# Sketched attention and a gated FFN on one core: weight loads in thirds, a two-step release of the later loads, casts and fills moved to ScalarE

## The chip, the cores and the metric

The kernel runs on 1 core of one Trainium2 chip. A core has TensorE (PE; its weight loads are shown as PEld), VectorE (DVE), ScalarE (ACT), GpSimd (POOL) and SyncE (SP), which issues transfers, and 16 DMA engines that carry all transfers. SP and ACT issue transfers whose descriptors are made by hardware; POOL's are made by its software and may change the type on the way. The metric is device microseconds of one execution, as the median of several runs.

## What is computed

Attention with a sketched kernel in place of the softmax, for 4 batches of 4 heads, 1088 positions and 32 dimensions, and behind it a gated FFN over 4352 tokens. In short:

```python
def phi(x):                                   # r = 8, so 64 features
    a = np.einsum('rd,bhsd->bhsr', S1, x)
    b = np.einsum('rd,bhsd->bhsr', S2, x)
    return np.einsum('bhsi,bhsj->bhsij', a, b).reshape(*x.shape[:-1], r * r)
q_p, k_p = (phi(q), phi(k))
kv = np.einsum('bhsf,bhsd->bhfd', k_p, v)
z = np.sum(k_p, axis=2)
num = np.einsum('bhsf,bhfd->bhsd', q_p, kv)
den = np.einsum('bhsf,bhf->bhs', q_p, z)[..., None] + 1e-06
attn = num / den
x = attn.transpose(0, 2, 1, 3).reshape(4352, 128)
gate = np.maximum(x @ w_gate, 0.0)            # w_gate, w_val: 128 x 1536
val = x @ w_val
out = gate * val @ w_out                      # w_out: 1536 x 128
```

All inputs and the output are float32 in memory; the FFN and the large products run in float16.

## The kernel before

Everything but the loads at the start is a `Task`: an engine, an expected time that the engine is taken (`occ`) and until the result is there (`lat`), tasks that it needs (`deps`) or only follows (`after`), PSUM banks, and an expected earliest time (`at`). `Plan.set_due` gives each task a due time, counted back from those of the FFN units with a slack of 200 ns at each step, and `Plan.run` puts the tasks in an order by list scheduling over the expected times: for each engine the task that can start first, or among those within 30 ns the one due first. The instructions are then written in that order. So all expected times (the `land` table of loads, `at`, `due`) only shape the order on each engine; on the chip an instruction waits for its engine's earlier instructions and for its data, and for no clock. Changing an expected time can therefore move work anywhere in the program.

The stages, for each batch b:

- Keys: DVE transposes `k_sb` to `kt` (L405), PE multiplies by the sketch `sk` (L415, two products), DVE transposes the result to `abk` (L427), PE sums for z (L474) and forms the denominator's weights (L491, DVE zd and wst), POOL makes the 64 features `kp` (L301; for batch 0 DVE makes a part, from a copy of `abk` in PSUM that ACT makes, L448), PE multiplies by `v_sb` (L513), and DVE puts the result into `kv_bd` (L528).
- Queries, in groups (batch 0 in chunks of 1, 1, 2 and 4, batches 1 to 3 in 8, one rest group at the end): DVE transposes `q_sb` to `qt` (L588, L590), PE multiplies by `wst` (L612), DVE transposes to `abq` (L627), bw, dn, rd and an normalise, DVE or POOL makes the features `qp` (L301), which are turned to `pt` by PE and ACT (L671, L712; batch 0 and the rest group) or by a transposing DMA (L701; batches 1 to 3), PE multiplies by `kv_bd` (L678, "num"), and ACT writes `xT` (L720).
- FFN, 102 units of 512 columns: PE multiplies by `wg` and `wv` (L747), ACT takes the relu (L758), DVE multiplies (L767), PE multiplies by `wo` (L778, "out"), and ACT evicts each finished group (L795), whose store SP issues.

Until the first FFN matmul, PE's planned gaps are filled with products of zeros (L824).

The loads. SP issues the first sketch half, k of batch 0 in two parts and q of batch 0 in one. POOL fills batch 1's constant parts (`fills`, L291 to L295: zeros in `wst`, the unused end of `v_sb`, of `kt` and `kv_bd`), issues v of batch 0, `wg` and `wv` whole, makes `kp` of batch 0, issues `wo` (L367), and fills for batches 2 and 3. The k and q of batches 1 to 3 are issued by SP, one behind the other, once POOL has written one element into `k_sb` of batch 1 (the gate):

```python
def e_gate(t):
    nc.gpsimd.memset(k_sb[1][0:1, 0, 0:1], 0.0)
    for b in range(1, B):
        load_pairs(nc.sync, k_sb[b], k, b)
        load_pairs(nc.sync, q_sb[b], q, b)
P.add("gate", "POOL", 70, 100, emit=e_gate, at=T_GATE).due = T_GATE
```

The v of batches 1 to 3 are issued by POOL among its arithmetic, and cast to float16 on the way.

Of the kernel before, what the change touches and what calls it, by code (L numbers as in the profile page):

```python
# [9 lines left out]
FP32 = mybir.dt.float32  # L10
# [28 lines left out]
class Plan:  # L39
# [4 lines left out]
    def __init__(self, free, a_max, f_max, n_banks):  # L44
        self.tasks = []
        self.free = dict(free)
        self.a_max, self.f_max, self.n_banks = a_max, f_max, n_banks
        self.sem = 45.0

    def add(self, *args, **kw):  # L50
        t = Task(*args, **kw)
        self.tasks.append(t)
        return t

    def set_due(self, slack):
        after = {}
        for t in self.tasks:
            for d in t.deps + t.after:
                after.setdefault(id(d), []).append(t)
        order, seen = [], set()  # L60

        def visit(t):
            stack = [(t, iter(after.get(id(t), ())))]
            seen.add(id(t))
            while stack:
                top, it = stack[-1]
                for n in it:
                    if id(n) not in seen:
                        seen.add(id(n))
                        stack.append((n, iter(after.get(id(n), ()))))  # L70
                        break
                else:
                    order.append(top)
                    stack.pop()

        for t in self.tasks:
            if id(t) not in seen:
                visit(t)
        for t in order:
            for n in after.get(id(t), ()):  # L80
                s = slack if n.kind != "f" or t.kind != "f" else 0.0
                t.due = min(t.due, n.due - t.lat - s)

    def run(self, first_f):
# [97 lines left out]
def kernel(  # L182
# [12 lines left out]
    nc = tc.nc  # L195

    B, H, S, D = q.shape
# [8 lines left out]
    CB = C - CA  # L206
    NG = 10
    NH = 14
    assert (B, H, D, R, C) == (4, 4, 32, 8, 17)

    ctx.enter_context(tc.manual_schedule())
# [11 lines left out]
    k_sb = [const.tile([128, 2, C * D], FP32, name=f"k_sb{b}") for b in range(B)]  # L223
    q_sb = [const.tile([128, 2, (C + 1) * D], FP32, name=f"q_sb{b}") for b in range(B)]
    v_sb = [const.tile([128, H, CA * D], FP16, name=f"v_sb{b}") for b in range(B)]
    wg = const.tile([DM, NJ, 128], FP16, name="wg")
    wv = const.tile([DM, NJ, 128], FP16, name="wv")
    wo = const.tile([128, NJ, DM], FP16, name="wo")

    def load_pairs(eng, dst, src, b, hp=None):  # L230
# [3 lines left out]
        else:  # L234
            eng.dma_start(out=dst[:, hp, 0:C * D], in_=x[:, hp])

    def load_v(eng, dst, b):
        x = v[b].rearrange("h (t c) d -> t h (c d)", c=C)
        eng.dma_start(out=dst[0:T], in_=x[:, :, 0:CA * D])
        eng.dma_start(out=dst[T:128, :, 0:CB * D], in_=x[:, :, CA * D:])  # L240
# [5 lines left out]
    load_pairs(nc.sync, q_sb[0], q, 0)  # L246

    zero = const.tile([128, 128], FP16, name="zero")
    nc.vector.memset(zero, 0.0)  # L249
# [38 lines left out]
        nc.vector.memset(maskkv[64 * p:64 * p + 64, p], KVSCALE)  # L288
    nc.vector.tensor_tensor(out=maskz, in0=mz2[:, 0], in1=mz2[:, 1], op=ALU.add)

    def fills(eng, b):  # L291
        eng.memset(wst[b], 0.0)
        eng.memset(v_sb[b][T:128, :, CB * D:], 0.0)
        eng.memset(kt[b][:, :, C], 0.0)
        eng.memset(kv_bd[b], 0.0)  # L295

    fills(nc.vector, 0)

    def outer(eng, dst, a, b):
        n = dst.shape[1]  # L300
# [4 lines left out]
            op=ALU.mult,  # L305
        )

    T0, STEP, T_GATE, T_DT = 12500.0, 830.0, 12500.0, 2500.0
    P = Plan(free={"PE": 1200.0, "ACT": 3100.0, "DVE": 3600.0, "POOL": 3000.0, "SP": 20000.0},
             a_max=3, f_max=5, n_banks=7)  # L310

# [6 lines left out]
    def pool(n):  # L318
        return dict(occ=70 + 1.86 * n, lat=120 + 1.86 * n)

    T_S = 4000.0
    land = dict(k00=4200.0, k01=4850.0, q0=6700.0, v0=8700.0, wg=10500.0, wv=13000.0, wo=16500.0,
                k1=17500.0, v1=20000.0, q1=20500.0, k2=22500.0, v2=23000.0, q2=24500.0, k3=26500.0,
                v3=26000.0, q3=28500.0)


    def e_st(t):
# [26 lines left out]
    t_w0 = [P.add("wst0", "ACT", 350, 480, deps=[t_st], after=[t_sk], emit=e_wst0, frees=[t_st])]  # L354

    def prep(b):
        f = P.add(f"fill{b}", "POOL", 800, 800, emit=lambda t: fills(nc.gpsimd, b))
        t_fill.append(f)
# [3 lines left out]
    t_fill = []  # L362
    t_w0 += [prep(b) for b in range(1, B)]


    def e_load(dst, src):
        return lambda t: nc.gpsimd.dma_start(out=dst, in_=src)  # L367

    l_v0 = P.add("ld_v0", "POOL", 1350, 1350, emit=lambda t: load_v(nc.gpsimd, v_sb[0], 0))
    l_g = P.add("ld_wg", "POOL", 740, 740, deps=[l_v0],  # L370
                emit=e_load(wg, moe_w_gate.rearrange("m (j f) -> m j f", j=NJ)))
    l_v = P.add("ld_wv", "POOL", 560, 560, deps=[l_g],
                emit=e_load(wv, moe_w_val.rearrange("m (j f) -> m j f", j=NJ)))
    l_o = P.add("ld_wo", "POOL", 1050, 1050, deps=[l_v],
                emit=e_load(wo, moe_w_out.rearrange("(j f) m -> f j m", f=128)))
    l_v_sb = [l_v0]
    l_v0.after += t_fill[:1]
    for f in t_fill[1:]:
        f.after.append(l_o)
    prev = l_o  # L380
    for b in range(1, B):
        prev = P.add(f"ld_v{b}", "POOL", 1350, 1350, deps=[prev, t_fill[b - 1]],
                     emit=lambda t, b=b: load_v(nc.gpsimd, v_sb[b], b), at=10000.0 + 3000.0 * b)
        prev.due = T0 - 1000.0 + 5000.0 * b
        l_v_sb.append(prev)

    def e_gate(t):
        nc.gpsimd.memset(k_sb[1][0:1, 0, 0:1], 0.0)
        for b in range(1, B):
            load_pairs(nc.sync, k_sb[b], k, b)  # L390
            load_pairs(nc.sync, q_sb[b], q, b)

    P.add("gate", "POOL", 70, 100, emit=e_gate, at=T_GATE).due = T_GATE


    class Keys:
# [2 lines left out]
    kk = []  # L399
    for b in range(B):  # L400
        K = Keys()
        kk.append(K)

        def ke_t1(t, b, hp):
# [114 lines left out]
        m = None  # L519
        for lo, hi in cuts:  # L520
            x = P.add(f"k{b}kv{lo}", "PE", 60 * (hi - lo), 60 * (hi - lo) + 200,
                      deps=[K.phi[lo, 0], K.phi[lo, 1], *K.v], after=[m], banks=0 if m else 1)
            m = m or x
            x.emit = lambda t, b=b, lo=lo, hi=hi, m=m: ke_kv(t, b, lo, hi, m)
        K.kv = x
# [41 lines left out]
    for i, (bs, c0, n, r, o0) in enumerate(groups):  # L567
        G = Group()
        gg.append(G)
        G.bs, G.c0, G.n = bs, c0, n  # L570
        X = 4 * n
        rest = len(bs) > 1
        early = i < 2
        turned = not rest and bs[0] > 0
# [118 lines left out]
        for c in range(0, n, 4):  # L693
            p = Part()
            G.parts.append(p)
            p.G, p.n, p.c0, p.col = G, min(n, 4), c, col
            col += p.n * 128
            need = phi if n <= 4 else phi[2 * (c // 4):2 * (c // 4) + 2]
            if turned:
                def qe_dt(t, G=G, c=c):  # L700
                    nc.sync.dma_start_transpose(  # L701
                        out=G.pt[:, 2 * c:2 * c + 8],
                        in_=G.qp[:, 4 * c:4 * c + 16].rearrange("s x f -> s (x f)"))

                tre = P.add(f"q{i}dt{c}", "SP", T_DT, T_DT + 1500, deps=need, after=[last_dt],
                            emit=qe_dt)
# [12 lines left out]
            p.x = P.add(f"q{i}x{c}", "ACT", **act(128 * p.n), deps=[num], frees=[num],  # L719
                        emit=lambda t, p=p, f=num: nc.scalar.copy(  # L720
                            out=xT[:, p.col:p.col + p.n * 128], in_=ps[:, f.bank, 0:p.n * 128]))
            before.setdefault(id(r), []).append(p.x)
# [8 lines left out]
    for gi, p in enumerate(p for G in gg for p in G.parts):  # L731
# [3 lines left out]
        for i in range(NJ // per):  # L735
# [9 lines left out]
            def e_mm(t, w, p=p, js=js, W=W):  # L745
                for y, j in enumerate(js):
# [5 lines left out]
            vv = P.add(f"v{u}", "PE", 218, 218 + 170, deps=[p.x, g], banks=1, kind="f",  # L752
                       emit=lambda t, f=e_mm: f(t, wv), at=land["wv"])
            g.due, vv.due = due, due + 220

            def e_relu(t, U, g):
# [102 lines left out]
```

## Time and profile before

| what | us |
|---|---|
| runs shown | 110.37, 110.91, 111.2 (median 110.91) |
| profiled execution, its own time | 110.49 |
| its span | 108.7 |
| PE busy (92% of the span) | 99.8 |
| DVE busy (84%) | 91.6 |
| ACT busy (66%) | 72.2 |
| POOL busy (47%) | 51.1 |
| first FFN matmul starts | 12.89 |
| wg, wv, wo landed | 12.40, 14.24, 16.40 |
| k of batch 1 issued, landed | 12.45, 19.53 |

Times inside the execution are counted from the span's start. The granted clock of TensorE is 1.00 in every stretch up to 106 us. An engine's share of busy time is an average over a head in which loads set the pace and a long stretch of FFN units; a wait is charged to what the profile infers as the last releaser. L numbers are lines of the kernel before; in the changed kernel the same statements stand 13 to 27 lines lower (L747 is L774, L778 is L805, L405 is L425).

### The profile page before, as it was taken

How to read it: one execution, taken by the hardware profiler on the slowest of the kernel's cores; microseconds unless marked ns; L12 is line 12 of the kernel's file. 1: busy time of each engine (PE TensorE's matmuls, PEld its weight loads, DVE VectorE, ACT ScalarE, POOL GpSimd, SP SyncE). 2: the span in 40 equal slices, each digit the busy share in tenths (PEclk: the TensorE clock that was granted, in tenths of full speed). 3: DMA queues.
4: the chain of work that ended last, by engine and by line, in shares of the span. 5: the costliest groups of instructions: out<-in, count | busy, mean ns of one | idle time of the engine just before them, and what ended most of it. 6: DMA issues, size and time to landing. Idle time of an engine off the chain costs nothing.

```text
span 108.7 us, 3081 instructions
## 1 busy us (share of the span) xinstructions
PE 99.8 (92%) x1175; PEld 66.7 (61%) x1175; DVE 91.6 (84%) x199; ACT 72.2 (66%) x140; POOL 51.1 (47%) x84
## 2 busy tenths in 40 slices
PE   6999978599999999999999999999999999999930
PEld 6778767187657554656576556565774666568710
DVE  4659973899999998999999799799995999889820
ACT  4330469168597619666978495499767989989910
POOL 6979898089829719503294088025925000000000
PEclk9999999999999999999999999999999999999997
DMA  1999999999912582100045440000471400400302
GB/s 38 319 184 158 156 221 300 309 310 311 222 31 48 103 99 54 42 0 6 0 96 113 86 96 3 0 0 11 106 148 30 103 0 0 99 1 6 82 14 48
DMA packets 14559, 10.75 MB, mean 99 GB/s; under 512 B 8657, under 2 KB 11345, under 8 KB 14545
## 3 DMA queue, kind: packets, MB, share of 16 engines
q1 hardware_dynamic: 10328, 8.20, 29.3%
q0 software_dynamic: 4016, 2.29, 15.5%
q8 instruction: 9, 0.15, 0.5%
q10 hardware_dynamic: 200, 0.07, 0.3%
q14 instruction: 6, 0.04, 0.1%
HBM read 9.05 MB, written 2.23 MB: 104 GB/s over the span
## 4 chain that ended last, share of the span: by engine, by line
PE 68%; DMA 16%; DVE 6%; POOL 3%; ACT 1%; SPq 1%; issue 1%; DVEq 1%
PE ps L747 37%; PE ps L778 18%; DMA k_sb<-in_k_dram 7%; DMA q_sb<-in_q_dram 5%; DMA pt<-qp 4%; PE ps L678 3%; PE ps L612 3%; PE ps L415 2%; POOL qp L301 2%; PE ps L474 2%; DVE kp L301 1%; ACT xT L720 1%; PE ps L513 1%; DVE abq L627 1%; DVE qt L588 1%
## 5 line engine op out<-in xcount | busy, mean ns | idle before, releaser
L758 ACT ACTIVATE g_sb<-ps 128x512 f16<-128x512 f32 x102 | 57.2, 602 | 16.3 <-PE ps L747 14.7
L767 DVE TENSOR_TENSOR ht<-g_sb,ps 128x512 f16<-128x512 f16 x102 | 63.9, 676 | 4.2 <-ACT g_sb L758 1.5
L778 PEld LDWEIGHTS <-ht 128*128 128x128 f16 x408 | 29.5, 98 | 17.8 <-DVE ht L767 4.1
L778 PE MATMUL ps<-wo,ht 128*128 128x128 f16 x408 | 39.1, 219 | 0.4 <-DVE ht L767 0.4
L747 PE MATMUL ps<-xT,wv 128*128 128x512 f16 (+2 forms) x132 | 36.6, 331 | 0.8 <-DMA wv<-in_moe_w_val_dram 0.8
L747 PE MATMUL ps<-xT,wg 128*128 128x512 f16 (+2 forms) x132 | 35.6, 330 | 0.6 <-ACT xT L720 0.5
L301 POOL TENSOR_TENSOR kp<-abk 128x640 f16<-128x640 f32 (+1 forms) x14 | 16.3, 1193 | 8.2 <-DVE abk L427 8.2
L301 POOL TENSOR_TENSOR qp<-an,abq 128x512 f16<-128x512 f32 x16 | 16.7, 1070 | 0.5
L747 PEld LDWEIGHTS <-wv 128*128 128x128 f16 x132 | 11.4, 98 | 4.6 <-issue 1.4
L747 PEld LDWEIGHTS <-wg 128*128 128x128 f16 x132 | 11.7, 98 | 3.7 <-issue 1.7
L637 POOL TENSOR_TENSOR bw<-abq 128x128 f32<-128x128 f32 (+1 forms) x9 | 3.8, 424 | 14.0 <-DVE abq L627 13.7
L720 ACT CAST xT<-ps 128x512 f16<-128x512 f32 (+2 forms) x11 | 5.4, 488 | 5.4 <-PE ps L678 5.4
L824 PE MATMUL ps<-zero 128*128 128x128 f16 x84 | 7.7, 250 | 1.1 <-DVE zero L249 1.1
L405 DVE STREAM_TRANSPOSE kt<-k_sb 128x544 f32<-128x544 f32 x8 | 5.6, 726 | 2.9 <-DMA k_sb<-in_k_dram 2.9
L654 POOL TENSOR_TENSOR an<-abq,rd 128x256 f32<-128x256 f32 (+2 forms) x6 | 2.9, 480 | 9.4 <-DVE rd L651 9.3
L824 PEld LDWEIGHTS <-zero 128*128 128x128 f16 x84 | 6.1, 113 | 1.7 <-DVE zero L249 1.1
L627 DVE STREAM_TRANSPOSE abq<-ps 128x512 f32<-128x512 f32 (+2 forms) x11 | 6.3, 577 | 0.8 <-PE ps L612 0.7
L795 ACT ACTIVATE o_sb<-ps 128x512 f32<-128x512 f32 (+2 forms) x11 | 5.5, 501 | 2.0 <-PE ps L778 1.9
L415 PE MATMUL ps<-kt,sk 64*64 64x288 f32 x64 | 5.4, 425 | 1.6 <-DVE kt L405 1.6
L678 PE MATMUL ps<-pt,kv_bd 128*128 128x512 f16 (+2 forms) x20 | 5.1, 337 | 0.3 <-DMA pt<-qp 0.2
L612 PE MATMUL ps<-qt,wst 64*64 64x256 f32 (+3 forms) x112 | 5.1, 303 | 0.0
L427 DVE STREAM_TRANSPOSE abk<-ps 128x320 f32<-128x320 f32 (+1 forms) x8 | 3.4, 460 | 1.9 <-PE ps L415 1.8
(75 smaller groups left out, 64.4 us busy)
## 6 DMA issues: line engine op xcount, KB each, us to landing
q_sb<-in_q_dram SPq DMA_DIRECT2D x4, 544.0 KB, 8.8
out_dram<-o_sb SPq DMA_DIRECT2D x14, 128.0 KB, 2.3
k_sb<-in_k_dram SPq DMA_DIRECT2D x3, 544.0 KB, 8.6
v_sb<-in_v_dram POOLq DMA_DIRECT2D x4, 144.0 KB, 8.6
k_sb<-in_k_dram SPq DMA_DIRECT2D x2, 272.0 KB, 2.7
v_sb<-in_v_dram POOLq DMA_DIRECT2D x4, 128.0 KB, 10.1
wg<-in_moe_w_gate_dram POOLq DMA_DIRECT2D x1, 384.0 KB, 7.2
wv<-in_moe_w_val_dram POOLq DMA_DIRECT2D x1, 384.0 KB, 8.5
```

The source lines that it names most:

```text
L301: eng.tensor_tensor(out=dst.rearrange("s x (i j) -> s x i j", i=R), in0=a[:, :, :, None].to_broadcast([128, n, R, R]), in1=b[:, :, None, : ...
L405: nc.vector.transpose(kt[b][:, hp, 0:C].rearrange("p c t -> p (c t)"), k_sb[b][:, hp])
L415: nc.tensor.matmul(ps[64 * st:64 * st + 64, first.bank + h2, 0:CA * 32], sk[r, 64 * hp:64 * hp + 64], kt[b][r, hp, CA * st:CA * st + CA].r ...
L612: nc.tensor.matmul(o, wst[G.bs[0]][r, hp].rearrange("p a f -> p (a f)"), G.qt[r, hp, st], start=True, stop=True, skip_group_check=True)
L627: nc.vector.transpose(G.ab[:, lo:hi].rearrange("p x h f -> p h x f"), ps[:, f.bank:f.bank + 2, lo * 32:hi * 32].rearrange("p h (x t) -> p ...
L678: nc.tensor.matmul(o, kv_bd[G.bs[0]][:, 2 * hp:2 * hp + 2].rearrange("f a d -> f (a d)"), G.ptc[:, hp, c0:c0 + n], start=hp == 0, stop=hp ...
L720: emit=lambda t, p=p, f=num: nc.scalar.copy(out=xT[:, p.col:p.col + p.n * 128], in_=ps[:, f.bank, 0:p.n * 128]))
L747: nc.tensor.matmul(ps[:, t.bank, y * W:(y + 1) * W], w[:, j], xT[:, p.col:p.col + W], start=True, stop=True)
L758: nc.scalar.activation(out=U.g_sb, in_=ps[:, g.bank], func=ACTF.Relu)
L767: nc.vector.tensor_tensor(out=U.ht, in0=U.g_sb, in1=ps[:, vv.bank], op=ALU.mult)
L778: nc.tensor.matmul(ps[:, OB, s * DM:(s + 1) * DM], U.ht[:, y * n * 128 + s * 128:y * n * 128 + (s + 1) * 128], wo[:, j], start=(j == 0 and ...
L824: nc.tensor.matmul(ps[:, OB, 0:128], zero, zero, start=True, stop=True)
```

## The change

- `wg` and `wv` are loaded in thirds of their 12 blocks (g, v, g, v, g, v), each a transfer of POOL's, all six ahead of the `kp` of batch 0. An FFN unit's matmuls wait for the third that they read.
- `wo` is issued behind `kp` as before, but now ahead of every later q and v load: the gate is split. The first gate is a one-element copy on ScalarE that releases k of batch 1; the second, on POOL behind the issue of `wo`, releases q and v of batch 1 and then k, q and v of batches 2 and 3.
- The v of batches 1 to 3 come as float32 (`v32`) through SP's queue, and ScalarE casts each in two halves (L532 of the changed kernel).
- The fills of batches 1 to 3 are made by ScalarE, as copies of a zero, at the start.
- q of batch 0 is loaded in four pieces: the first four chunks of both halves, then the rest.
- The slack per step is 500 ns instead of 200 for keys of batches 2 and 3 and for query groups from the sixth on, and expected times (`land`, `T_GATE`, `T_DT`) are others, so that the order on each engine differs after the head. Among other things, the product of batch 2's z now stands right behind batch 1's num, batch 3's num comes at FFN unit 71 (72 before), and the rest group at unit 84 (72 before).

```diff
-    def set_due(self, slack):
+    def set_due(self):
...
-                s = slack if n.kind != "f" or t.kind != "f" else 0.0
+                s = t.slack if n.kind != "f" or t.kind != "f" else 0.0
...
+    def load_q0(eng, part):
+        x = q[0].rearrange("(x y) (t c) d -> (y t) x (c d)", y=2, c=C)
+        for st in range(2):
+            lo = (CA * st + (Q0 if part else 0)) * D
+            hi = (CA * st + (Q0 if not part else CB if st else CA)) * D
+            eng.dma_start(out=q_sb[0][:, :, lo:hi], in_=x[:, :, lo:hi])
...
-    def fills(eng, b):
-        eng.memset(wst[b], 0.0)
-        eng.memset(v_sb[b][T:128, :, CB * D:], 0.0)
-        eng.memset(kt[b][:, :, C], 0.0)
-        eng.memset(kv_bd[b], 0.0)
+    def fills(b):
+        for x in (wst[b], (v32[b] if b else v_sb[b])[T:128, :, CB * D:], kt[b][:, :, C], kv_bd[b]):
+            if b == 0:
+                nc.vector.memset(x, 0.0)
+            else:
...
+                nc.scalar.copy(out=x, in_=z.to_broadcast(shape))
...
-    T0, STEP, T_GATE, T_DT = 12500.0, 830.0, 12500.0, 2500.0
+    T0, STEP, T_GATE, T_DT, SLACK = 12500.0, 830.0, 10600.0, 1700.0, 500.0
...
-        f = P.add(f"fill{b}", "POOL", 800, 800, emit=lambda t: fills(nc.gpsimd, b))
+        f = P.add(f"fill{b}", "ACT", 950, 1050, emit=lambda t: fills(b), after=[t_w0[0]])
...
+    prev = l_v0
+    for y in range(3):
+        js = slice(y * JT, (y + 1) * JT)
+        for n, dst, src in (("wg", wg, moe_w_gate), ("wv", wv, moe_w_val)):
+            prev = P.add(f"ld_{n}{y}", "POOL", 570, 570, after=[prev],
+                         emit=e_load(dst[:, js], src.rearrange("m (j f) -> m j f", j=NJ)[:, js]))
...
+    def e_gate1(t):
+        nc.scalar.copy(out=k_sb[1][0:1, 0, 0:1], in_=zero[0:1, 0:1])
+        load_pairs(nc.sync, k_sb[1], k, 1)
+
+    def e_gate2(t):
+        nc.gpsimd.memset(q_sb[1][0:1, 0, 0:1], 0.0)
         for b in range(1, B):
-            load_pairs(nc.sync, k_sb[b], k, b)
+            if b > 1:
+                load_pairs(nc.sync, k_sb[b], k, b)
             load_pairs(nc.sync, q_sb[b], q, b)
-
-    P.add("gate", "POOL", 70, 100, emit=e_gate, at=T_GATE).due = T_GATE
+            load_v(nc.sync, v32[b], b)
+
+    gate1 = P.add("gate1", "ACT", 180, 240, emit=e_gate1, at=T_GATE)
+    gate1.due = T_GATE
+    P.add("gate2", "POOL", 70, 100, emit=e_gate2, at=T_GATE + 2500.0, after=[gate1]).due = T_GATE
...
+        P.slack = 200.0 if b < 2 else SLACK
...
-        K.v = [P.add(f"v{b}", "POOL", 1, 1, deps=[l_v_sb[b]], at=land[f"v{b}"])]
+        if b == 0:
+            K.v = [l_v0]
+        else:
+            K.v = [P.add(f"v{b}{x}", "ACT", **act(2 * CA * D), at=land[f"v{b}"], emit=lambda t, b=b, x=x:
+                         nc.scalar.copy(out=v_sb[b][:, 2 * x:2 * x + 2], in_=v32[b][:, 2 * x:2 * x + 2]))
+                   for x in range(2)]
...
+        P.slack = 200.0 if i < 5 else SLACK
...
             g = P.add(f"g{u}", "PE", 218, 218 + 170, deps=[p.x], banks=1, kind="f",
-                      emit=lambda t, f=e_mm: f(t, wg), at=land["wg"])
+                      emit=lambda t, f=e_mm: f(t, wg), at=land[f"w{max(js) // JT}"])
...
-    P.set_due(200.0)
+    P.set_due()
```

More of the change, by code (lines that the diff above doesn't have):

```diff
@@ L48, in __init__ @@
         self.sem = 45.0
+        self.slack = 200.0
     def add(self, *args, **kw):
         t = Task(*args, **kw)
+        t.slack = self.slack
         self.tasks.append(t)
         return t
-    def set_due(self, slack):
+    def set_due(self):
         after = {}
@@ L208 @@
     NH = 14
+    Q0 = 4
+    JT = NJ // 3
     assert (B, H, D, R, C) == (4, 4, 32, 8, 17)
@@ L225 @@
     v_sb = [const.tile([128, H, CA * D], FP16, name=f"v_sb{b}") for b in range(B)]
+    v32 = [const.tile([128, H, CA * D], FP32, name=f"v32_{b}") if b else None for b in range(B)]
     wg = const.tile([DM, NJ, 128], FP16, name="wg")
@@ L245 @@
     load_pairs(nc.sync, k_sb[0], k, 0, 1)
-    load_pairs(nc.sync, q_sb[0], q, 0)
+    load_q0(nc.sync, 0)
+    load_q0(nc.sync, 1)
     zero = const.tile([128, 128], FP16, name="zero")
@@ L289 @@
     nc.vector.tensor_tensor(out=maskz, in0=mz2[:, 0], in1=mz2[:, 1], op=ALU.add)
-    def fills(eng, b):
-        eng.memset(wst[b], 0.0)
-        eng.memset(v_sb[b][T:128, :, CB * D:], 0.0)
-        eng.memset(kt[b][:, :, C], 0.0)
-        eng.memset(kv_bd[b], 0.0)
-    fills(nc.vector, 0)
+    def fills(b):
[3 more added lines that the diff above has]
+            else:
+                shape = list(x.shape)
+                z = zero[128 - shape[0]:128, 0:1]
+                for _ in shape[2:]:
+                    z = z.unsqueeze(1)
+                nc.scalar.copy(out=x, in_=z.to_broadcast(shape))
+    fills(0)
     def outer(eng, dst, a, b):
@@ L321 @@
     T_S = 4000.0
-    land = dict(k00=4200.0, k01=4850.0, q0=6700.0, v0=8700.0, wg=10500.0, wv=13000.0, wo=16500.0,
-                k1=17500.0, v1=20000.0, q1=20500.0, k2=22500.0, v2=23000.0, q2=24500.0, k3=26500.0,
-                v3=26000.0, q3=28500.0)
+    land = dict(k00=3900.0, k01=4700.0, q0=7400.0, v0=8800.0, w0=10100.0, w1=11400.0, w2=12700.0,
+                wo=16000.0, k1=16500.0, q1=19000.0, v1=21000.0, k2=22500.0, q2=24500.0,
+                v2=26000.0, k3=28000.0, q3=29500.0, v3=31500.0)
     def e_st(t):
@@ L356, in prep @@
     def prep(b):
-        f = P.add(f"fill{b}", "POOL", 800, 800, emit=lambda t: fills(nc.gpsimd, b))
-        t_fill.append(f)
+        f = P.add(f"fill{b}", "ACT", 950, 1050, emit=lambda t: fills(b), after=[t_w0[0]])
         return P.add(f"prep{b}", "ACT", **act(64), deps=[t_w0[0], f], emit=lambda t: nc.scalar.copy(
             out=wst[b][:, :, :, 0:2 * R], in_=wst[0][:, :, :, 0:2 * R]))
-    t_fill = []
     t_w0 += [prep(b) for b in range(1, B)]
@@ L369 @@
     l_v0 = P.add("ld_v0", "POOL", 1350, 1350, emit=lambda t: load_v(nc.gpsimd, v_sb[0], 0))
[L370 to L374, printed above, removed]
-                emit=e_load(wo, moe_w_out.rearrange("(j f) m -> f j m", f=128)))
[L376 to L388, printed above, removed]
+    prev = l_v0
[4 more added lines that the diff above has]
+                         emit=e_load(dst[:, js], src.rearrange("m (j f) -> m j f", j=NJ)[:, js]))
+            prev.due = 2000.0 if y < 2 else 8000.0
+    l_v0.due = 2000.0
+    l_o = P.add("ld_wo", "POOL", 1050, 1050, after=[prev],
+                emit=e_load(wo, moe_w_out.rearrange("(j f) m -> f j m", f=128)))
+    l_o.due = 8500.0
+    def e_gate1(t):
[3 more added lines that the diff above has]
+        nc.gpsimd.memset(q_sb[1][0:1, 0, 0:1], 0.0)
         for b in range(1, B):
-            load_pairs(nc.sync, k_sb[b], k, b)
+            if b > 1:
+                load_pairs(nc.sync, k_sb[b], k, b)
             load_pairs(nc.sync, q_sb[b], q, b)
-    P.add("gate", "POOL", 70, 100, emit=e_gate, at=T_GATE).due = T_GATE
+            load_v(nc.sync, v32[b], b)
+    gate1 = P.add("gate1", "ACT", 180, 240, emit=e_gate1, at=T_GATE)
+    gate1.due = T_GATE
+    P.add("gate2", "POOL", 70, 100, emit=e_gate2, at=T_GATE + 2500.0, after=[gate1]).due = T_GATE
     class Keys:
@@ L521 @@
             x = P.add(f"k{b}kv{lo}", "PE", 60 * (hi - lo), 60 * (hi - lo) + 200,
-                      deps=[K.phi[lo, 0], K.phi[lo, 1], *K.v], after=[m], banks=0 if m else 1)
+                      deps=[K.phi[lo, 0], K.phi[lo, 1], *K.v], after=[m], banks=0 if m else 1,
+                      at=land[f"v{b}"])
             m = m or x
@@ L703, in qe_dt @@
                         in_=G.qp[:, 4 * c:4 * c + 16].rearrange("s x f -> s (x f)"))
-                tre = P.add(f"q{i}dt{c}", "SP", T_DT, T_DT + 1500, deps=need, after=[last_dt],
+                tre = P.add(f"q{i}dt{c}", "SP", T_DT, T_DT + 1800, deps=need, after=[last_dt],
                             emit=qe_dt)
@@ L750 @@
             g = P.add(f"g{u}", "PE", 218, 218 + 170, deps=[p.x], banks=1, kind="f",
-                      emit=lambda t, f=e_mm: f(t, wg), at=land["wg"])
+                      emit=lambda t, f=e_mm: f(t, wg), at=land[f"w{max(js) // JT}"])
             vv = P.add(f"v{u}", "PE", 218, 218 + 170, deps=[p.x, g], banks=1, kind="f",
-                       emit=lambda t, f=e_mm: f(t, wv), at=land["wv"])
+                       emit=lambda t, f=e_mm: f(t, wv), at=land[f"w{max(js) // JT}"])
             g.due, vv.due = due, due + 220
```

## The prediction

> **What bounds the kernel now.** I read the chain of work that ended last first, then the busy times by stretch, PE's waits, and the timeline of the first 22 us. Of the chain (start, length, what), these pieces matter; nearly all the others are PE at its full pace:
>
> ```profile
> 12.45 7.08 DMA k_sb<-in_k_dram
> 19.55 0.76 DVE kt L405
> 20.35 1.34 PE ps L415 x16
> ...
> 32.02 0.35 DVE rd L651
> 32.45 0.64 POOL an L654
> 33.16 2.11 POOL qp L301 x2
> 35.28 4.60 DMA pt<-qp
> 39.92 0.61 PE ps L678 x2
> 40.55 0.59 ACT xT L720
> ```
>
> So the first FFN work runs dry behind batch 1's keys (issued 12.45, landed 19.53), and the FFN work of batch 0 ends just as batch 1's first xT comes (41.15). The busy times (stretch, length, then PE, PEld, DVE, ACT, POOL, clock, DMA share, GB/s) tell where engines are idle:
>
> ```profile
> 12.00:14.00 2.00, 1.46 (x21) 1.05 (x18) 1.97 (x8) 1.31 (x5) 1.91 (x6) 1.00 1.25 152
> 14.00:16.00 2.00, 1.71 (x35) 1.44 (x35) 1.34 (x5) 1.36 (x3) 1.79 (x4) 1.00 1.45 220
> 16.00:18.00 2.00, 1.87 (x35) 1.75 (x32) 1.30 (x3) 1.61 (x4) 1.48 (x4) 1.00 1.11 292
> 18.00:20.00 2.00, 0.80 (x13) 0.60 (x10) 0.45 (x1) 1.36 (x4) 1.04 (x2) 1.00 1.17 310
> 20.00:22.00 2.00, 1.65 (x22) 0.78 (x23) 2.00 (x6) 0.00 (x0) 0.06 (x1) 1.00 1.17 310
> 22.00:40.00 18.00, 17.70 (x208) 11.75 (x206) 17.94 (x35) 12.13 (x22) 12.68 (x14) 1.00 0.72 163
> ```
>
> From 12 to 22 us PE is idle 2.51 us and DVE 2.94; from 22 to 40 both are full, and DVE is the fuller. All sixteen DMA engines are full up to 28 us: the order of the transfers decides when FFN work may start. PE's named waits (total, times, longest) agree:
>
> ```profile
> PE ps L415 <- DVE kt L405: 1.6, 1, 1.6
> ...
> PE ps L747 <- DMA wv<-in_moe_w_val_dram: 0.8, 1, 0.8
> PE ps L747 <- ACT xT L720: 0.5, 2, 0.2
> ```
>
> And the four POOL instructions that the change moves, by the timeline:
>
> ```profile
> 5.18 0.58 POOL L367 DMA_DIRECT2D wg<-in_moe_w_gate_dram  x1
> ...
> 7.04 2.53 POOL L301 TENSOR_TENSOR kp<-abk 128x640 f16<-128x640 f32 x2 [0.73 <-DVE abk L427]
> ...
> 9.52 1.09 POOL L367 DMA_DIRECT2D wo<-in_moe_w_out_dram  x1
> ...
> 12.34 0.09 POOL L388 MEMSET k_sb<- 1x1 f32 x1
> ```
>
> Times are against the profiled execution, 110.49 us with a span of 108.7. The median of the runs shown is 110.91, 0.42 more; I add that at the end.
>
> **The head, to the first FFN matmul (12.89 before).** POOL loses batch 1's fills (2.94 to 3.80) and starts the v load at 2.95: 0.78 + 0.62 for v, then six weight loads instead of two, at 0.57 each (both old ones have 128 rows, so have the thirds) 3.42, ends at 7.77. Queued behind are the two kp, which started at 7.04: 0.73 later, ending 10.30, and behind them the issue of wo, 10.35 to 11.45. PE's kv matmuls (9.52 before) wait for kp until 10.35; they take 0.60 to issue, eight fillers 0.49, so the next q product starts at 11.45 instead of 11.12. The first FFN matmul moves by +0.33, to 13.2. Nothing else in the head costs, if covered: ScalarE gets eight fill copies and two prep copies between 5.64 and 7.32. Nearest rows: 128x64 0.24, 128x128 0.27, 128x256 0.38 alone, which is 1.16 a batch end to end; the FFN relu shows 0.48 from one start to the next against 0.60 alone, so overlapped about 0.7 to 0.95. I take 0.85: the copy of abk (L448) is about 0.1 late. At 1.16 it would be 1.1 late, DVE's two kp with it, and what is past 0.33 + 0.27 of slack, 0.5, would be paid. q0 in four pieces brings its first part before 7.29, when DVE is free (it waited 0.3 until 7.56); that is lost in PE's later q product.
>
> **The wait for wv (0.8) goes.** Units 0 to 2 take a third each, and PE reaches the last third about 15.2; in the run before both whole weights had landed by 14.24.
>
> **The loads.** The key gate is now a 1-element copy on ScalarE behind the fills. Nothing on the chip holds it until its planned 10.6: ScalarE gets there about 9, so k1 is issued about 9.1 instead of 12.45, ahead of wo on the engines. The second gate stays behind the wo issue on POOL, so q1, v1 and the rest are issued from 11.6. What PE waits for is now wo: in its order come g and v of three units, a q product, a transpose, one num, and then the first out matmul, with everything behind it. Without waits that is 13.2 + 0.61 + 0.55 + 0.67 + 0.29 + 0.45 + 0.28, about 16.1. wo landed at 16.40 before. It gets k1 in front: in the trace's packet records a 2176-byte packet takes 88 to 101 ns, 16 an engine, 1.5 us. q0's 512-byte pieces: records of 512-byte packets show 27 to 29 ns, four for one of 88, 16 times, +0.45. Packets of thirds fall between those of wo (41 ns for 256 bytes written) and the whole weights (248 for 3072): +0 to +0.7. So wo lands at 16.40 + 1.5 + 0.45 + about 0.1 = 18.4, if k1 alone comes between; at 16.9 if the weights keep the engines and k1 follows, 1.5 later at about 18.5, where DVE would win the same 1.0 (19.55 before).
>
> How the queues share an engine is the open point. The records show k1's first packet at 14.10, in the same 4 ns as an earlier transfer's end on that engine, and none before, though it was issued at 12.45; later k1, v1, q1, v1, k2, v2 land in turn (19.53, 20.71, 21.64, 22.73, 23.96, 24.96): whole transfers of the two queues alternate. The Trainium skill's "DMA: Bandwidth & Descriptors" (Queues, rings and completion order) says that each engine goes round between its queues a packet at a time; by it each third would pay for one load of q, k or v, and the time would be that of the slower rival below. Against turns from the start stands a row: engines which ended wv at 13.58 and 13.95 went on to wo with k1 issued over 1.1 us before: what is already lined up is served first. I take k1 alone in between.
>
> **What 18.4 is worth.** PE: out 0.22, transposes 0.45, g 0.44, v 0.22, out 0.22, v 0.22, num 0.27, then k1's product 1.30, ending 21.74 at (g, v, out units) 5, 5, 2; before it ended 21.69 at 6, 5, 3. That is 0.05 + 0.44 behind; equal at wo = 17.9. DVE: its transposes of k1 are done while PE waits, so its next mult starts 1.6 after wo (out, transposes, g, relu 0.60), at 20.0 instead of 21.03: 1.0 ahead, equal at 19.4. Up to batch 1's num PE needs 18 g, 19 v (0.216 each) and 19 outs (0.22), 12.2, and z 0.70, tr 0.45, w 0.23, num 0.43, q product 1.02, kv 0.52, k2 product 1.30, 4.65: 16.8 of the 18.2 it had. So 1.4 is slack there, and DVE and the chain behind it decide: 0.5 behind on PE is paid from it, and 1.0 is won by xT at 41.15. After num the new order puts k2's z (0.70) into the wait for xT, where PE idled 0.23 in 40 to 42, and batch 3's num at units 71, 70, 67 instead of 72, 72, 70, so the 0.23 idle at 82 to 84 (xT after num, nothing else left) goes: 0.4 together. Against it six casts of v on ScalarE, 0.54 each by the relu's spacing: 3.2 us, into 5.87 idle between 22 and 40. Bounds 0 (idle time) and 1.6 (half of each passed on to DVE, which starves behind the relus); I take 0.2. Each cast also holds the relus behind it until v has landed; v1 is due about 21.7, its cast about 22.4. POOL's six v issues (about 0.65 each, 12.8 to 19) go; POOL waited in 12 to 22 and nothing is gained.
>
> Sum: 110.49 - 1.0 - 0.4 + 0.2 = 109.3; on the scale of the median 109.7. Own range: wo at 17.6 with free casts wins 1.7 + 0.4, 108.8; wo at 19.0 with casts at 0.8 gives back all, 110.9.
>
> **Rivals.** (1) Slower: the queues take turns from the moment k1 is there, a third against a load. On a late engine (v0 at 8.6 us, a third 0.7, loads 1.5, v halves 0.8): two transfers of thirds, k1, a third, a third, q1, a third, v1, a third, v1, 17.4, then wo 2.6, is 20.0; with a stall of 1.6, such as single packets of the weights had in the records at 8.3 to 8.7, more loads slip in and it is 24. PE and DVE stand until then: past 19.4 each us costs one. With the 0.4 won late and 0.2 for the casts, on the median's scale 110.9 + 0.6 - 0.2 = 111.3 to 110.9 + 4.6 - 0.2 = 115.3, centre 113.2. It makes the kernel slower from wo landing at 19.6 on, by over 1% from 20.7. For: the landings in turn; against: wo kept k1 off. (2) Faster still: the long packets of 1.6 do not come again, so that wo lands at 16.8 with k1 before it. PE is then 1.1 ahead and has 1.4 of slack, 2.5 in all, DVE 2.6: 110.9 - 2.5 - 0.2 = 108.2. For: half of the engines ended wv at 11.5 without them; against: nothing in the change touches them but the size of a transfer. (3) The gain is given back: the relus stand behind a cast whose v has not landed, or ScalarE's fills are 1.16 a batch; the 1.3 won goes, 110.2 to 111.4. (4) That thirds do nothing because the first unit waits for all weights is excluded: each third has its own wait in PE's order.
>
> **How the numbers follow.** Mine 0.45, (1) 0.25, (2) 0.12, (3) 0.18. A change of 1% is about what a measurement of this kernel can tell: under 109.8 is faster, over 112.0 slower. Mine gives 0.35 faster and 0.10 within; (2) faster; (3) within; (1) 0.03 within and 0.22 slower, and 0.03 of (3) may be slower. Faster 0.47, same 0.28, slower 0.25. The range goes from 108.0 (nearly half of rival 2 is left out) to 113.3 (nearly half of rival 1).
>
> **What would show it.** First FFN matmul near 13.2; k1 issued near 9.1; no wait for wv; PE's longest wait at an out matmul (L805), ended by wo near 18.4; no idle DVE before kt of batch 1; xT of batch 1 near 40.1; no gap at 82. Wrong if wo lands past 19.4, if relus wait behind L532, or if k1 is issued after 10.5.

## The result, and the profile after

The changed kernel takes 118.64 us (median of four runs, 117.51 to 119.19) where the kernel before took 110.64 in the same session: a ratio of 1.071, with a 95% interval of 1.061 to 1.080. It is slower by 8 us, 5 us past the upper end of the range that was given. The profiled execution took 118.51 with a span of 116.8 (before: 110.49 and 108.7). Runs of one kernel scatter: a ratio is formed from the faster runs alone (those within some 1.5% of the fastest), a median from all, and two kernels scatter so widely that no ratio is given for them.

The chain of work that ended last in the changed kernel (start, length, what) has three long transfers in it, `wo` and two transposes (the chain before had one transpose, at 35.28, and no `wo`):

```profile
8.19 2.48 POOL kp L319 x2
10.67 11.70 DMA wo<-in_moe_w_out_dram
22.40 0.59 PE ps L805 x4
23.42 1.28 PE ps L774 x12
25.98 1.73 PE ps L435 x16
...
41.75 4.59 DMA pt<-qp
...
82.45 4.49 DMA pt<-qp
```

`wo` was issued at 10.67 and landed at 22.37: 11.7 us, against 6.9 before (9.52 to 16.40). The busy times around its landing (stretch, length, then PE, PEld, DVE, ACT, POOL, granted clock, DMA share, GB/s):

```profile
16.00:18.00 2.00, 1.70 (x32) 1.19 (x29) 2.00 (x5) 1.60 (x5) 1.54 (x3) 1.00 1.22 296
18.00:20.00 2.00, 0.00 (x0) 0.00 (x0) 2.00 (x5) 0.05 (x1) 0.24 (x1) 1.00 1.16 213
20.00:22.00 2.00, 0.00 (x0) 0.00 (x0) 0.18 (x1) 0.00 (x0) 0.00 (x0) 0.59 1.12 216
22.00:24.00 2.00, 1.60 (x16) 1.59 (x16) 0.00 (x0) 0.55 (x2) 0.00 (x0) 0.50 1.01 357
24.00:26.00 2.00, 2.00 (x21) 1.59 (x23) 1.19 (x3) 1.03 (x3) 0.27 (x1) 0.50 1.11 194
26.00:28.00 2.00, 2.00 (x23) 1.07 (x24) 0.56 (x2) 0.37 (x1) 1.92 (x3) 0.71 1.10 220
```

Two things are to be seen. PE does nothing from 18 to 22. And the clock, the third number from the right, is at one half from 22 to 26: by the clock's own record in the trace it falls at 20.35, while PE stands, and rises at 27.18, when PE has long been at work again. PE's waits name two places that cost (total, times, longest):

```profile
PE ps L805 <- DMA wo<-in_moe_w_out_dram: 4.7, 1, 4.7
PE ps L705 <- DMA pt<-qp: 1.7, 2, 1.1
```

The balance of the 8.1 us of span: PE is idle 4.2 us longer, and busy 103.7 us instead of 99.8. Of these 3.9, 2.1 lie ahead of the first FFN matmul (13.9 against 11.8), of which more below, and 1.8 behind it (89.8 against 88.0, for the same products). In the rows above PE was busy 4.8 us at half clock, of which at most half, 2.4, is lost; so the half clock behind the wait for `wo` cost some 1.8 to 2.4 us.

### The profile page after: what moved, and what is told of

The parts are those of the page before. It is cut to its first block, busy times and chain, and to the rows that moved or that the text cites. A ratio compares the mean times of both kernels' runs of the same rounds, so it can differ in the third digit from the quotient of the medians.

```text
span 116.8 us, 3095 instructions
## 1 busy us (share of the span) xinstructions
PE 103.7 (89%) x1172; PEld 69.3 (59%) x1172; DVE 92.3 (79%) x199; ACT 78.6 (67%) x159; POOL 47.4 (41%) x70
## 4 chain that ended last, share of the span: by engine, by line
PE 64%; DMA 18%; POOL 7%; issue 3%; DVE 2%; DVEq 1%; ACT 0%; POOLq 0%
PE ps L774 30%; PE ps L805 16%; DMA wo<-in_moe_w_out_dram 10%; DMA pt<-qp 8%; PE ps L435 4%; POOL qp L319 4%; PE ps L851 3%; PE ps L705 3%; PE ps L639 3%; POOL kp L319 2%; PE ps L494 2%; POOL an L681 1%; PE ps L698 1%; DVEq L881 1%; DVE abq L654 1%
## 5 line engine op out<-in xcount | busy, mean ns | idle before, releaser
L794 DVE TENSOR_TENSOR ht<-g_sb,ps 128x512 f16<-128x512 f16 x102 | 64.7, 676 | 9.8 <-PE ps L774 6.6
L785 ACT ACTIVATE g_sb<-ps 128x512 f16<-128x512 f32 x102 | 58.1, 603 | 15.0 <-PE ps L774 11.9
L774 PE MATMUL ps<-xT,wv 128*128 128x512 f16 (+2 forms) x132 | 38.1, 336 | 0.0
L774 PE MATMUL ps<-xT,wg 128*128 128x512 f16 (+2 forms) x132 | 36.5, 336 | 0.0
L774 PEld LDWEIGHTS <-wg 128*128 128x128 f16 x132 | 12.2, 101 | 3.3 <-issue 1.1
L774 PEld LDWEIGHTS <-wv 128*128 128x128 f16 x132 | 12.0, 101 | 2.1 <-issue 0.4
L739 ACT COPY pt<-ps 128x256 f16<-128x256 f16 (+2 forms) x5 | 2.9, 583 | 9.5 <-PE ps L698 9.5
L851 PE MATMUL ps<-zero 128*128 128x128 f16 x81 | 8.3, 266 | 1.1 <-DVE zero L262 1.1
L435 PE MATMUL ps<-kt,sk 64*64 64x288 f32 x64 | 6.9, 535 | 0.0
## 6 DMA issues: line engine op xcount, KB each, us to landing
k_sb<-in_k_dram SPq DMA_DIRECT2D x3, 544.0 KB, 10.2
```

The source lines that it names most:

```text
L435: nc.tensor.matmul(ps[64 * st:64 * st + 64, first.bank + h2, 0:CA * 32], sk[r, 64 * hp:64 * hp + 64], kt[b][r, hp, CA * st:CA * st + CA].r ...
L774: nc.tensor.matmul(ps[:, t.bank, y * W:(y + 1) * W], w[:, j], xT[:, p.col:p.col + W], start=True, stop=True)
L785: nc.scalar.activation(out=U.g_sb, in_=ps[:, g.bank], func=ACTF.Relu)
L794: nc.vector.tensor_tensor(out=U.ht, in0=U.g_sb, in1=ps[:, vv.bank], op=ALU.mult)
L851: nc.tensor.matmul(ps[:, OB, 0:128], zero, zero, start=True, stop=True)
```

## The experiments

A ratio is to runs of the kernel before on the same chip.

### First theory: `wo` has to share the DMA engines, so let the loads wait for it

Theory 1 was that q1 and v1 (the q and v of batch 1), released behind the issue of `wo` but before its landing, take the engines from it. In the first two kernels the later loads wait for the landing itself, by a small transfer that reads `wo` ahead of them on SP's queue. The edit of the first is below; in the second k1 stands behind it too:

```diff
 def e_gate2(t):
-    nc.gpsimd.memset(q_sb[1][0:1, 0, 0:1], 0.0)
+    nc.sync.dma_start(out=tell, in_=wo[0:1, 0])
```

> The changed kernel, but the second step (q1, v1, and all of k2 to v3) is released by the landing of wo and no longer by a POOL fill behind wo's issue; k1 is still released early. Theory 1 (q1 and v1 share the DMA engines with wo's 256-byte packets, so wo lands 6 us late; PE stands 4.7 us at the first out product and then runs 5 to 7 us at half clock): wo lands at 15.5 to 17, no granted half clock between 20 and 27, time 118.5 - 4.7 - 2.4 = 111.4, give or take 0.8 (109.3 if the clock also rises as early as before). Rival (the loss lies in the new order, ScalarE's casts and fills and the slow head, and the wait for wo only hides it): wo lands early all the same, but the time stays above 115. Price of the experiment: q1 and v1 are issued some 5 us later, about 16.8; if batch 1 then waits, idle time stands before its v product.

> As the first, but k1 also stands behind wo's landing: one release for all later loads, as in the kernel before, only later. Theory 1: wo lands about 15, k1 at 18 to 18.5, time 111 to 112, no better than the first, since k1 alone in front of wo cost little. Rival (k1 ahead of wo is a large part of the delay): 1 us or more better than the first one.

Measured: 116.17 us for the first (ratio 1.067, 1.052 to 1.082), 116.5 for the second (1.063, 1.024 to 1.101). `wo` lands at 18.06 and 17.26, much earlier, as theory 1 said, if later than the 15 to 17 it gave; the 4.7 us wait shrinks to 1.0 and to nothing; and the time falls by only 0.4 to 0.8% of the kernel before. By what was written down, the rival has it: there is a second loss, which the wait for `wo` hid. (Part of it may be the price of the experiments, which issue q1 and v1 some 7 us later; in the runs with the fills undone, below, q1 is 2.6 later.) ScalarE's row in time for the first of these kernels shows where (start, length, line, operation, count, idle time ahead of it and what ended it):

```profile
22.20 1.09 ACT L786 ACTIVATE g_sb<-ps 128x512 f16<-128x512 f32 x2
26.27 1.24 ACT L533 CAST v_sb<-v 128x576 f16<-128x576 f32 x2 [2.98 <-DMA v<-in_v_dram]
27.42 0.59 ACT L786 ACTIVATE g_sb<-ps 128x512 f16<-128x512 f32 x1
```

The cast of batch 1's v stands in ScalarE's stream at its planned place. When v is late, ScalarE waits 3.0 us for it, and the relus behind it wait too; PE then waits for a relu, and the clock is halved from 29.10 to 32.51:

```profile
PE ps L775 <- ACT g_sb L786: 2.6, 1, 2.6
```

In the changed kernel no cast waited: PE stood for `wo` until 22.4, v1 had landed at 23.25, and its casts came at 29.71. The second kernel had its loss elsewhere: PE waited 3.4 us for the transposes of k1 (L436 on L426), which was issued only at 17.95.

> The kernel before with one edit: the gate and value weights come in thirds, by six issues of POOL. Everything else (one gate at 12.5, v by POOL's casting loads, q0 whole, fills on POOL) as before. My prediction's own step: the 0.8 us wait for wv goes, the head grows by 0.3; 110.0 to 110.9. Rival (the six issues hold POOL and the head long enough to cost by themselves): above 112.

The edit puts the six issues of thirds in place of the two whole weights. Measured: 110.89 (1.018, 1.002 to 1.033; by the medians of all runs 1.009), a little slower if anything. The wait for `wv` is gone, as expected, and nothing is won by it. So the thirds are not where 8 us went.

> The changed kernel with k1 put into the second step, both right behind wo's issue: one gate. Theory 1: q1 and v1 still share the engines with wo, which lands at 19 to 22; 116 to 119. Rival (k1's early release is what delays wo): wo lands before 18 and the time falls under 114.

The edit moves k1's issue from `e_gate1` into `e_gate2`. Measured: 116.61 as a median, with runs from 112.35 to 118.72; in the profiled one (118.64) `wo` took 12.3 us and PE waited 6.7 for it. The early k1 is not needed for the delay of `wo`, since without it the delay is as long. The same kernel took 112 in one run and 119 in two; what was different in the run at 112, which left no profile, is not shown.

### Second theory: the lead that `wo` has over the next load

POOL issues `wo` and then, in the kernel before, makes eight fills ahead of the gate (its issue at 9.52 and the gate at 12.34 stand in the prediction):

```profile
10.60 0.23 POOL L292 MEMSET wst<- 128x128 f32 x1
...
12.09 0.30 POOL L295 MEMSET kv_bd<- 128x256 f16 x1
...
12.45 0.37 SPq L233 DMA_DIRECT2D k_sb<-in_k_dram  x1
```

The change moved these fills to ScalarE. So it took away a delay of 1.7 us between `wo` and the loads that follow:

```profile
10.67 1.09 POOL L383 DMA_DIRECT2D wo<-in_moe_w_out_dram  x1
11.75 0.09 POOL L403 MEMSET q_sb<- 1x1 f32 x1
...
11.87 0.37 SPq L238 DMA_DIRECT2D q_sb<-in_q_dram  x1
```

From the start of `wo`'s issue to that of the first load behind it (k1 in the kernel before, q1 here) it was 2.9 us; now it is 1.2. One kernel gives the changed one a delay back, one takes it from the kernel before:

```diff
 def e_gate2(t):                             # changed kernel, gate later
+    for _ in range(7):
+        nc.gpsimd.memset(idle, 0.0)
     nc.gpsimd.memset(q_sb[1][0:1, 0, 0:1], 0.0)
...
 def e_wo_gate(t):                           # kernel before, gate earlier
     nc.gpsimd.dma_start(out=wo, in_=moe_w_out.rearrange("(j f) m -> f j m", f=128))
+    e_gate(t)
```

> The changed kernel with seven small POOL fills of a scratch tile (about 1.8 us, as long as the fills that stood in this place before the change) between wo's issue and the second release; all orders are as in the changed kernel. Theory 2 (the lead that wo has over the next loads decides: 2.8 us in the kernel before, 1.2 us in the changed one, because the fills went to ScalarE): q1 is issued at 13.6 instead of 11.87, wo lands at 17.5 to 19 instead of 22.4, and the loads that follow are not put off as by a wait for the landing; no half clock at 20 to 27, time 112 to 114. Rival (wo shares the engines whenever the loads are released before it has landed, as theory 1 of the first four had it): wo still lands past 20 and the time stays above 116.

> The kernel before with its one gate moved ahead of the eight POOL fills, directly behind wo's issue: 1.7 us sooner, nothing else moved. Theory 2: k1 and q1 are issued at 10.7 to 11.2, wo lands at 19 to 22 instead of 16.4, PE stands 3 to 5 us at the first out product and loses clock behind it; 114 to 118. Rival (something else of the change makes wo late: the thirds, the split of q0, the v loads in fp32): 110 to 111.5 with wo under 18.

Measured: the changed kernel with the delay, 115.22 as a median (112 to 114 was expected) and 1.027 (1.017 to 1.038) against before; q1 was issued at 14.36 (the fills took more than planned, a lead of 3.7) and `wo` landed at 18.50. The kernel before without the delay: 116.21 as a median, from 111.5 to 117.4, where it took 110.77 as it stood. The profiled run happens to be the 111.5, and even there `wo` took 9.0 us and PE waited for it:

```profile
PE ps L781 <- DMA wo<-in_moe_w_out_dram: 1.8, 1, 1.8
```

The three runs at 116 to 117 left no profile, so that `wo` was later still in them is inferred. Moving one POOL instruction ahead of eight others, with nothing else touched, costs the kernel before 0.7 us in its best run and 5.4 at the median. Theory 2 stands: the lead, given back or taken away, moves `wo` and the time in both kernels. With the lead given back, the second cause shows again in the changed kernel: in the profiled run (117.1) ScalarE's casts waited 4.3 us for v, and PE 3.9 for relus.

> The changed kernel with the later v loads as before the change: three casting loads by POOL behind wo, in wo's own queue, without the ScalarE casts; gates and thirds as changed. Theory 2: q1, k2, q2 still follow wo by 1.2 us on the other queue, wo lands at 19 to 22 and the time stays at 115 to 118. Rival (the fp32 v loads of q1's queue are what takes the engines from wo): wo under 18, time under 113.

The edit gives POOL its three casting loads back, behind `wo` in its own queue, and drops the casts. Measured: 119.32 (1.080, 1.076 to 1.084), `wo` landing at 24.28. The fp32 loads of v are not what holds `wo` up: k and q alone on SP's queue do it just as well (POOL's v loads stand behind `wo` in its own queue). All profiles together, by the lead (start of `wo`'s issue to start of the next load's issue; an early k1, issued ahead of `wo`, is not counted) and by how long `wo` took from issue to landing:

| lead, us | kernels | wo took, us |
|---|---|---|
| 1.2 | changed; one gate; v by POOL; before, gate early; the two with fillers | 11.7; 12.3; 13.6; 9.0; 13.5 and 12.1 |
| 2.9 | before; before with slack (twice); before with v by ScalarE | 6.9; 6.9 and 7.2; 7.0 |
| 3.7 to 3.8 | changed, gate later; fills undone; third part undone (three profiles) | 7.8; 7.2; 6.3, 7.2 and 6.4 |
| 5.3 or after landing | thirds alone; all wait; next loads wait | 6.3; 6.6; 7.4 |

At 1.2 us `wo` takes 9.0 to 13.6 us, at 2.9 some 7, and past 2.9 there is little more to win; no run has a lead in between. The records of `wo`'s 1536 packets say how: in the changed kernel and in the one with the later gate the median packet starts at the same time (15.15 and 15.14 us), but the last at 21.03 against 17.96. Only the tail is late, and the landing comes behind the last packet. Why the tail is kept back so long, the runs don't show.

### What the half clock costs

```diff
 def e_out(t, U, js=js, n=n, first=not outs):
+    for _ in range(100 if first else 0):
+        nc.tensor.matmul(ps[:, OB, 0:128], zero, zero, start=True, stop=True)
```

> The changed kernel with 60 filler products of zeros (3.4 us at full clock) on TensorE directly ahead of the first out product, where it stood idle for 4.7 us; loads as in the changed kernel. If the half clock after the wait comes from the idle time: no half clock between 20 and 27, and the time falls by what it cost, 2.4 us, to 115.5 to 116.7. If the granted clock goes by something else: still 118 to 119, or more by up to 1 where wo lands before the fillers end.

> As the run with 60 filler products ahead of the first out product, with 100 (5.7 us at full clock), since 60 ended 4.5 us before wo came. If idle time is what halves the clock: the rest of the wait is under 2.6 us, no half clock between 20 and 30, 115.5 to 117. If the clock falls all the same: 118 to 120.

With 60 fillers nothing was told apart: 118.17 (1.066, 1.061 to 1.071), where 115.5 to 116.7 was expected. In the profiled run the head was early and `wo` came at 23.58, so that PE still stood 4.5 us behind the fillers and the clock fell as before. With 100: 116.35 (1.047, 1.033 to 1.062). PE's row shows the fillers in the place of the wait, and the clock of the whole span (40 slices, tenths) below it holds:

```profile
17.65 5.75 PE L804 MATMUL ps<-zero 128*128 128x128 f16 x100
23.23 0.39 PE L807 MATMUL ps<-wo,ht 128*128 128x128 f16 x4
```

```profile
PEclk9999999999999999999999999999999999999997
```

The loads came as late as in the changed kernel (`wo` at 22.80), the first out product started 0.8 later, and the kernel is 2.4% faster by the two ratios (their intervals just meet): some 2.6 us, against the 1.8 to 2.4 from the trace. The half clock is a result of the idle time, and a quarter to a third of the loss.

### The third part, undone in halves and whole

> The kernel before with v1 to v3 loaded in fp32 on SP's queue (order k, q, v of each batch) and cast by ScalarE, the fills left on POOL: wo's lead of 2.8 us stays. Theory 3: wo lands at 16 to 17 as before, v1 lands at 23 to 25, the casts wait for it in ScalarE's stream and the relus behind them: 1 to 4 us of idle PE between 22 and 36, with half clock behind it where it is over 2.6 us; 112 to 116. Rival (the casts do no harm where wo is on time): 110 to 111.5.

Here the kernel before gets only the v path of the change: v in fp32 on SP's queue, in the order k, q, v, and the casts on ScalarE. Measured: 118.33 (1.061, 1.049 to 1.073), above the 112 to 116 expected and nearly as bad as the whole change, with `wo` landing in 7.0 us. ScalarE's row in time, in the profiled run:

```profile
20.82 0.28 ACT L799 ACTIVATE o_sb<-ps 128x128 f32<-128x128 f32 x1
25.23 0.67 ACT L511 CAST v_sb<-v 128x576 f16<-128x576 f32 x1 [4.13 <-DMA v<-in_v_dram]
25.81 1.08 ACT L762 ACTIVATE g_sb<-ps 128x512 f16<-128x512 f32 x2
...
31.98 0.67 ACT L511 CAST v_sb<-v 128x576 f16<-128x576 f32 x1 [3.39 <-DMA v<-in_v_dram]
...
37.46 0.67 ACT L511 CAST v_sb<-v 128x576 f16<-128x576 f32 x1 [2.36 <-DMA v<-in_v_dram]
```

Each batch's first cast waits, 9.9 us in all, and the clock is halved twice behind it. (Its order was planned with the kernel before's landing times, in which v1 is there at 20.0; it landed at 24 and later.)

> The changed kernel without its third part: the fills are POOL's again and stand between wo's issue and the second release (all three sets, 2.6 us), and the later v loads are POOL's casting loads behind wo; thirds, the split of q0, the early k1 and the slack as changed. Theory 3 (two causes: wo's lead of 1.2 us, and v casts that stand ahead of relus in ScalarE's stream and wait for loads that are late): both are gone, wo lands at 17 to 18.5, no relu waits behind a cast, no half clock in the middle; 110 to 112. Rival (the thirds, the early k1 or the slack cost several microseconds too): above 113.

> The changed kernel without its third part, in five rounds. If thirds, early k1 and slack add up: 108.5 to 109.2, below the slack alone. If the slack carries all: 109.2 to 109.6, the same as the slack alone.

> The changed kernel with only the fills undone: POOL fills between wo's issue and the second release (2.6 us), v still loaded in fp32 on SP's queue and cast by ScalarE. Theory 3: wo lands at 17 to 18.5, but casts wait for v in ScalarE's stream and relus behind them; 113 to 117, as with the dummy fills. Rival (the fills alone were the cause, the dummies only cost POOL time): 109 to 111.5.

In the first two the fills are POOL's again, between `wo` and the second gate, and v comes by POOL; in the third only the fills are undone. Measured: 109.37 (0.989, 0.981 to 0.998) and, in five rounds, 109.1 (0.986, 0.981 to 0.991) for both halves undone; 112.82 (1.011, 1.003 to 1.018; by the medians of all runs 1.025) with the fills undone alone. With the changed kernel and the run of v by POOL this is a table of ratios to the kernel before:

| | fills on ScalarE | fills on POOL, ahead of the second gate |
|---|---|---|
| v in fp32, cast by ScalarE | 1.071 | 1.011 |
| v by POOL's casting loads | 1.080 | 0.986 |

The fills carry 6 to 9 points of it. The v path costs 2.5 points where `wo` is on time (3.4 by the medians of all runs), and nothing where it is late: one wait hides the other. With both undone the loss is gone, and what is left of the change makes the kernel 1.1 and 1.4% faster than before in two sessions. These are all the waits of PE that the profile names (the first is the start of the program):

```profile
PE ps L852 <- DVE zero L262: 1.1, 1, 1.1
PE ps L806 <- DVE ht L795: 0.4, 2, 0.2
PE ps L706 <- DMA pt<-qp: 0.3, 1, 0.3
```

and its busy times in the stretch that counted, where PE had idled 2.51 us before:

```profile
12.00:22.00 10.00, 9.87 (x176) 8.14 (x174) 9.79 (x28) 6.01 (x17) 8.27 (x23) 1.00 1.22 287
22.00:40.00 18.00, 17.74 (x212) 11.67 (x209) 17.58 (x35) 12.68 (x23) 15.73 (x18) 1.00 0.73 142
```

### The other parts by themselves

> The kernel before with the change's slack and transpose times alone (slack 500 for late batches, the DMA transposes planned at 1.7 and 3.5 us). The changed kernel's trace shows PE waits of 1.7 us on pt transposes at 46 and 87, against 0.2 in the kernel before. If the slack brings those: 111 to 112.5, with waits on pt. If they come only from the delays ahead of them: 109.3 to 110.8, the 0.4 that my prediction gave the slack or nothing.

> The kernel before with the slack and transpose figures alone, in five rounds: 108.8 to 109.8 if the 2% of the first three rounds holds, with an interval under 1; 110.3 to 110.8 if they were chance.

> The changed kernel without its third part (fills and later v as before the change) and without the slack and transpose figures: what is left is thirds, q0 in pieces and the early k1. My prediction's step gave these parts 0.8 to 1.0, so 109.5 to 110. Rival (the slack alone, which measured 2% by itself, carries the whole gain of the version with slack): no different from the kernel before, 110.4 to 111.2.

The slack and the transpose times alone, put into the kernel before, gave 0.980 (0.969 to 0.991) in three rounds, and 0.999 (0.994 to 1.003) in five: the first was chance, and there is no gain that can be told from none. Thirds, q0 in pieces and the early k1 without the slack gave 0.999 (0.994 to 1.003) too. All four together, in the version above, gave 0.986 in the same session. But the medians of all runs lie closer than these ratios: 109.10 for all four, 109.49 without the slack and 109.67 with the slack alone, where the kernel before had 110.06 with runs from 108.87 to 111.41. That the slack is worth something once the loads come earlier is a hint and not shown.

## Why the prediction was wrong

**The head, to 13.2.** Right as a sum, and blind to the clock. In two profiles of kernels with the changed kernel's head (one gate, 60 fillers), in which the clock rose to full at 3.9 and 4.9 us, the first FFN matmul came at 13.13. In the changed kernel's own profile the clock rose only at 10.11 (the record of the clock begins there, and the views show 1.00 ahead of it): the sixteen products of k0 took 2.20 us instead of 1.20, and the first FFN matmul came at 15.12. This is no effect of the change: the first rise lay between 3.9 and 10.3 us over the 18 profiles, early and late for versions of both kernels, and the kernel before with the slack also began its FFN at 15.01 in both of its profiles. It costs little at the end either (those had spans of 108.2 and 108.0), since the kernel before waits for loads in the stretch to 22 us anyway. In the changed kernel an early head only made PE wait longer for `wo`: 6.7 us in the run with one gate.

**The wait for `wv` goes.** It went, but as a step it was worth nothing that can be told: thirds alone 1.018, thirds with q0 in pieces and early k1 0.999. That the wait stood in a stretch whose length other loads set is the likely reason, and not shown by itself.

**k1 issued at 9.1.** It was 10.36: the fills on ScalarE took 1.1 us a batch, near the upper bound of 1.16 and not the 0.85 that was chosen, and the copy of `abk` stood between. With the fills back on POOL it was 9.04.

**`wo` at 18.4, "if k1 alone comes between".** This is the step that failed. The price of k1 (1.5, and 0.45 for q0) was rather too high: where `wo` kept its lead it took 6.6 us without k1 ahead and 6.3 to 7.8 with it. But q1 and v1 came between too. The prediction had the number in hand, q1 issued from 11.6, and the two rows of the timeline that it showed (issue of `wo` at 9.52, gate at 12.34) hold the lead of the kernel before. Of the fills that left POOL it counted those of batch 1, as time won in the head, and did not ask what those of batches 2 and 3 had been holding back: the second gate "behind the `wo` issue" was read as an order, where what counted was a distance. In place of 18.4, `wo` landed at 22.37; with the lead given back, at 16.95 to 18.50. One reading that spoke for "k1 alone" was also weak: that engines went on to `wo` at 13.58 and 13.95 with k1 issued at 12.45. In all 18 profiles the program's very first k load, with only the small load of the sketch ahead of it in its queue, has its first packet 0.98 to 1.02 us after its issue; if k1 takes the same, it had been at the engines for 0.1 and 0.5 us then, and not for over 1.1. So the row hardly shows that what is lined up is served first.

**Rival 1** named the right transfer (`wo` at 20 to 24) and the wrong mechanism: a third of the weights against a load from the moment k1 is there. In the trace the thirds landed 0.6 to 0.7 us apart, the last at 12.41, with k1 issued at 10.36; it was `wo` that was late, behind the issue of q1 and v1. (So it is in nine of the eleven profiles with k1 issued ahead of the last third's landing; in two there is a gap of 1.2 and 2.2 us, and the last lands at 13.84 and 14.06.) The page cited there, the Trainium skill's "DMA: Bandwidth & Descriptors" (Queues, rings and completion order), has the engines go round between queues; the profiles show both, thirds that are mostly not held up and a `wo` that is, so the rule by itself would not have given the time. Even the rival's slow end, 115.3, was 3.3 us short, most of which is what the clock took; for `wo` at 22.4 its price gives 113.7.

**What 18.4 is worth, slack and casts.** The idle stretches at 40 to 42 and 82 to 84 went, but came again as waits for transposes at 46 and 87 (1.7 us in all): the stalls moved with the delay. The casts took 0.67 to 0.78 each and some 0.57 from one start to the next; by this spacing, in which the prediction reckoned, that is 3.4 in all against the 3.2 that was put down. That they hold relus behind them until v has landed was named, with v1 due at 21.7; in the five profiles with v in fp32 and `wo` on time v1 came at 22.7 to 26.7, and in four of them casts waited for it or a later v, 2.6 to 9.9 us in all, with relus behind them (in the fifth, where all wait, k1 was later still). This was rival 3, sized at 1.3 us where it cost 2.5 points in the changed kernel with its fills undone, and with the v path put into the kernel before 6.

**The clock.** No step had a price for PE standing still beyond the standing itself. That was 1.8 to 2.6 of the 8 us.

## What to carry to other kernels

When work is moved off an engine that also issues transfers, look at what stood between its issues: the moved instructions may have been what kept a transfer (here one of 1536 small packets) ahead of the next ones, so compare the distance between the issues before and after, not their order. An instruction that waits for a load, put into the stream of an engine that feeds the critical one (here a cast ahead of relus), makes a late load a stall of everything, and it can stay hidden behind a longer wait until that one is mended. And give a wait of TensorE of some two microseconds or more a price beyond its length, because the clock can fall behind it: here 1.8 to 2.6 us on top of a wait of 4.7.

## What the runs showed of the hardware

- The clock fell after less idle time than the 2.6 us that the expectations went by. Cut into steps of 3.413 us from the first rise, and with the end of the program left out, the 18 profiles show a fall at the end of every step at full clock in which PE stood idle for 1.84 us or more (eight steps, 1.84 to 3.41), and at one with 1.58; eight steps with 1.07 to 1.66 of idle time kept the full clock. (At the end of the program it fell at 1.62 and more, and stayed at 1.34 and less.) In these places it stays at half for 3.4, 6.8 or 10.2 us. The Trainium skill's "TensorE: Matmul & The Clock Gate" (Part 1: The HAM clock gate) has a free-running window of 3413 ns, which these steps agree with, and puts the fall behind a whole idle window; here about half of a window was enough.
- The time of the first rise moves the head by 2 us from one execution to the next. Over eight profiles of kernels with the changed kernel's head, the first FFN matmul starts at 13.1 where the clock rose at 3.9 or 4.9, at 14.5 to 14.8 where it rose at 8.6 to 8.9, and at 15.1 to 15.2 where it rose at 10.1 to 10.3.
